# Packed queries times w_in in plain float32: eight side-by-side 64x32 tiles in place of three split products

## The chip, the cores and the metric

The kernel runs on one core of a Trainium2 chip (trn2). The metric is the device time of one launch in microseconds (us), taken as a median of several runs. The engines are named as in the profile: PE (TensorE matmuls), PEld (its weight loads), DVE (VectorE), ACT (ScalarE), POOL (GpSimd) and SP (SyncE, which issues all DMAs here).

## What is computed

```python
batch, n_heads, seq, head_dim, n_pack = 8, 8, 576, 64, 32          # d_model 512, d_ff 2048
def sm_attn(qq, kk, vv):
    s = scale * np.matmul(qq, kk.transpose(0, 1, 3, 2))
    a = np.exp(s - np.max(s, axis=-1, keepdims=True))
    a = a / (np.sum(a, axis=-1, keepdims=True) + 1e-09)
    return np.matmul(a, vv)
p_packed = sm_attn(p, k, v)                  # 32 packed queries per head
x = sm_attn(q, p_packed, p_packed)           # back to 576 rows per head
x = x.transpose(0, 2, 1, 3).reshape(4608, 512)
h = x @ w_in                                 # 512 x 2048
out = (0.5 * h * (1 + erf(h / sqrt(2)))) @ w_out
```

The weights arrive as 64-bit floating point numbers, so each 512-wide block of them is loaded as pairs of 32-bit words and put together on the chip ("decoded").

## The kernel before

Work goes by units. A unit u is one pair of batches (four pairs) and one 512-wide block of d_ff (four blocks), 16 units in all; u // 4 is the pair and u % 4 the block. The second attention's last product and w_in are joined the other way round: instead of (weights2 x p_packed) x w_in, the kernel first computes wp = p_packed x w_in, which has one row for each of 8 heads x 32 packed queries, and then h = wp-transposed-by-weights2 over those 256 rows. `hidden_steps` issues h in eight steps a unit (batch j = 0 or 1 of the pair, four 128-wide columns c), `gelu` evicts each and splits it, and `output_steps` multiplies it with w_out.

Most products run in TensorE's reduced float32 (F32R). So that no accuracy is lost, each operand is split into a high part (rounded to F32R) and a low part (the rest), and a product is made as three: high x high, high x low, low x high. `h` and `o` are of this kind. The attention scores (`products`, L483) are plain float32 in eight tiles of 64 rows by 32 columns of the array; unit 0's `wps` and `h` are plain float32 too.

For wp (`packed_w_in`), the packed queries of a head pair are laid out by `diagonals` in a 128x128 block-diagonal matrix `ph`, split by POOL (`packed_split`). Each unit has two groups (hh = 0, 1); a group makes, for two 128-row tiles of w_in, the three products of 512 columns, serves both batches of the pair at once, and lands in a two-bank PSUM tile of the ring `wide`. That ring holds two tiles, which `wps`, `h`, the scores and `o_edge` share. The result is evicted in four pieces of 64 rows by 512 columns: ACT casts a high part (L986), DVE subtracts it to get the low part (L990).

w_in is decoded in units 0 to 3, kept as a split tile `w` [128, 2, 512] (cast L935 on ACT, low part L884 on POOL), stored in DRAM (`ws`), and loaded again in units 4 to 15.

The order of all work is not the program's own: every operation is a generator step with a priority number and a cost, and `Order` runs a small model of the engines while the program is recorded, always issuing the ready operation with the lowest number. The tables FIRST (the first pair's attention and unit 0), LATER (the other three pairs) and LEAD hold these numbers. Before the first output product, the model fills PE's waits with dummy products (`keep_warm`, tile `idle<-still`), so that its clock stays up.

Of the kernel before, what the change touches and what calls it, by code (L numbers as in the profile page):

```python
# [10 lines left out]
F32 = mybir.dt.float32  # L11
F32R = mybir.dt.float32r
# [40 lines left out]
    "p": (-29.7, 4.9),  # L53
    "k": (11.1, 2.3, 11.3, 24.1),
    "v": (38.0, 41.0, 54.2, 58.2),
    "q": (26.8, 33.3, 45.5, 49.5),
    "scores1": (15.9, 4.7),
    "softmax1": (1.1, 16.6, -2.5, 19.8),
    "packed": (-28.0, 0.3, 2.2, 10.0),
    "scores2": (0.4, -12.1),  # L60
    "softmax2": (36.1, 29.5, 32.6, 41.4),
    "weights2": (25.3, 28.0, 35.5, 45.7),
# [4 lines left out]
LEAD = {"load": 4.4, "decode": -3.6, "packed_w_in": 4}  # L67

FIRST = {
    "p": (-200.0, -193.0),  # L70
    "k": (-186.0, -199.0, -185.0, -182.0),
    "v": (-195.0, -197.0, -181.0, -179.0),
    "q": (-183.0, -191.0, -178.0, -177.0),
    "w": (-187.0, -198.0, -194.0, -188.0, -192.0, -184.0, -190.0, -196.0, -189.0, -180.0, -176.0, -175.0),
    "scores1": (-29.0, -55.27, -22.89, -50.0),
    "softmax1": (-53.13, -50.0, -30.0, -29.0),
    "packed": (-48.76, -31.48, -27.58, -51.55),
    "scores2": (-51.65, -51.18, -34.07, -27.2),
    "softmax2": (-49.06, -48.66, -3.32, 1.29),
    "weights2": (-4.59, -15.04, -24.74, -16.37),  # L80
    "decode": (-45.0, -37.0, -20.64, -35.16, -36.53, -35.0, -50.97, -46.0, 1.0, 8.37, -33.0, 2.0),
    "packed_w_in": (-7.62, -48.76, -38.15, -25.99),
    "packed_split": (8.53, 1.15, 2.3, -11.78),
    "weights_split": (7.2, 1.11, -2.81, -0.07),
    "w_in_split": (-17.7, 3.0, 5.95, 3.0),
# [3 lines left out]
    "copy": ("DVE", "ACT", "DVE", "ACT", "ACT", "ACT", "DVE", "DVE"),  # L89
    "low": (0, 3, 4, 5),  # L90
    "banks": (False, False, False, False),
    "turn": {"k": ("ACT", "DVE", "ACT", "ACT"), "q": ("DVE", "DVE", "ACT", "ACT")},
# [42 lines left out]
class Op:  # L135
# [3 lines left out]
    def __init__(self, engine, cost, step, fn, takes=(), table=None, busy=True):  # L139
        self.engine, self.cost, self.step, self.fn = engine, cost, step, fn  # L140
        self.takes, self.table, self.busy = takes, table, busy


class Order:
# [4 lines left out]
    def __init__(self):  # L149
        self.now, self.serial, self.open = 0.0, 0, 0  # L150
        self.later, self.ready = [], {e: [] for e in (PE, ACT, DVE, POOL, DMA)}
        self.free = dict.fromkeys(self.ready, 0.0)
        self.table, self.link, self.under_way = None, DMA_FIRST, [0.0] * DMA_DEPTH
        self.warm, self.window, self.busy, self.idle = False, PE_WINDOW, 0.0, None
        self.free[PE] = PE_START
# [60 lines left out]
    def issue(self, engine):  # L216
# [23 lines left out]
        else:  # L240
            if op.table and op.table != self.table:
                self.table, begin = op.table, max(begin, self.free[engine] + TABLE_SWITCH)
            end = begin + op.cost
            if engine == PE:
                end = begin + self.clock(begin, op.cost, op.busy)
# [21 lines left out]
def packed_attention_gelu_ffn(ctx: ExitStack, tc: tile.TileContext, q, k, v, p, w_in, w_out, out):  # L267
# [40 lines left out]
    sms = ring("sm", 4, [P, S])  # L308
# [10 lines left out]
    wis = ring("wi", 4, [P, 2, FB], F32R)  # L319
    wos = ring("wo", 6, [P, 2, DM], F32R)  # L320
    wps = [ring("wp0", 1, [P, 2, 2, FB], F32R), ring("wp1", 2, [P, 2, 2, FB], F32R)]
# [6 lines left out]
    wos.names = [f"w_{u}_{i}" for u in range(NU) for i in range(4, 8)]  # L328
    gts.names = [f"g_{n}" for n in range(NU * 8)]
# [21 lines left out]
    ph = [const.tile([P, 2, 4 * P], F32R, name=f"ph{i}") for i in range(2)]  # L351
    for t in ph:
        nc.gpsimd.memset(t.bitcast(F32), 0.0)

    plain_ph = accs.take("ph")
    nc.gpsimd.memset(plain_ph, 0.0)


    pp_ready = {(b, hh): Event() for b in range(B) for hh in range(2)}
    plain_ready = {(b, hh): Event() for b in range(2) for hh in range(2)}  # L360
# [5 lines left out]
    a2T, plain_a2 = {}, {}  # L366
# [110 lines left out]
    def products(ts, lhs, rhs, swap=0):  # L477

        for n in range(2):
            rows = slice(64 * n, 64 * n + 64)  # L480
            for g in range(4):
                r0 = 32 * (g ^ 2 * swap)
                nc.tensor.matmul(  # L483
                    ts[n][r0:r0 + 32, :HALF], lhsT=lhs[n][rows, 32 * g:32 * g + 32], rhs=rhs(g)[rows],
                    start=True, stop=True)

    def scores_of_batch(bt, name, which, lhs, evacuate, engine, cost, step):
        xTs = [bt.xT[name, c].rearrange("p (g x) -> p g x", g=2) for c in range(2)]

        def part(half):  # L490
# [4 lines left out]
                    (t[:, 0], t[:, 1]), lhs, lambda g: xTs[g // 2][:, g % 2, cols], which == 2 and bt.j),  # L495
# [82 lines left out]
    def packed(s, step):  # L578
# [61 lines left out]
        s.ppT = yield Op(ACT, 0.16, step + 2, lambda t: nc.scalar.copy(t, bank(m)[:, :P]), [(ppts, f"ppT_{s.n}")])  # L640
        ring_.give(m)
        s.split = Event()
        if s.b < 2:
            yield Op(
                DVE, 0.2, step + 2,
                lambda: [nc.vector.tensor_copy(to[0], x) for to, x in diagonals(s, plain_ph.unsqueeze(1))])
            fire(plain_ready[s.b, s.hh])
            step = FIRST["packed_split"][s.i]
        start(packed_split(s, step + 2))

    def diagonals(s, base):

        j = s.bt.j
        for sel in range(2):
            rows = slice(64 * sel, 64 * sel + 64)
            yield [
                base[rows, part].rearrange("p (hh ea sel r) -> p hh ea sel r", hh=2, ea=4, sel=2)[
                    :, s.hh, j:4 - j:3 - 2 * j, sel] for part in range(base.shape[1])
            ], s.ppT[rows].rearrange("p (e sel r) -> p e sel r", e=2, sel=2)[:, :, sel]

    def packed_split(s, step):
        def fn():
            for (hi, lo), src in diagonals(s, ph[(s.b // 2) % 2]):
                nc.gpsimd.tensor_copy(hi, src)
                nc.gpsimd.tensor_tensor(lo, src, hi.bitcast(F32), ALU.subtract)

        yield Op(POOL, 1.4, step, fn)
        fire(s.split)
        fire(pp_ready[s.b, s.hh])

    def scores2_of_chunk(s, step):
# [4 lines left out]
            PE, 0.68, step, lambda *ts: products(banks(*ts), [s.ppT] * 2, lambda g: xT[:, g], s.bt.j), takes, busy=False)  # L676
        ts = ts if len(takes) > 1 else [ts]
        xts.give(s.bt.xT["q", s.hh])
        start(free_ppT(s))
# [9 lines left out]
    def scores2_of_batch(bt, step):  # L689
        for s in bt.chunks:  # L690
            s.e2 = yield Op(DVE, 0, step + 1, lambda t: None, [(sms, f"e2_{s.n}")])
        yield from scores_of_batch(
            bt, "q", 2, [s.ppT for s in bt.chunks],
            lambda s, cols, x: nc.vector.transpose(s.e2[:, cols], x), DVE, 0.74, step + 1)
        for s in bt.chunks:
            start(free_ppT(s))

    def free_ppT(s):
        yield s.split
        ppts.give(s.ppT)  # L700
# [19 lines left out]
    def softmax2(ss, step):  # L720
        n, m = len(ss), ss[0].mx2

        def centre(s):
# [3 lines left out]
                lambda: on(engine).tensor_tensor(u, u, per_block(m[:, 0, s.i]), ALU.subtract))  # L727
# [9 lines left out]
    def weights2(s, step):  # L737
# [8 lines left out]
        yield Op(engine, cost, step, lambda: on(engine).tensor_tensor(u, u, per_block(r), ALU.mult))  # L746
# [8 lines left out]
        else:  # L755
# [4 lines left out]
            engine, cost, step, lambda: on(engine).tensor_tensor(t[:, 1], raw, t[:, 0].bitcast(F32), ALU.subtract))  # L760
# [20 lines left out]

# [54 lines left out]
    def plain(u, i=0):  # L836

        return u == 0 and i < 4

    def parts_of(u, i=0):  # L840

        return 2 if plain(u, i) else 1

    w_ready = {(u, i, part): Event() for u in range(NU) for i in range(8) for part in range(parts_of(u, i))}
    wi_used = {(u, i): Event(0 if plain(u) else 1) for u in range(NU) for i in range(4)}
    plain_w, plain_used, plain_ph_used = {}, [Event(4) for _ in range(4)], Event(8)
    plain_ph_used.waiting.append(lambda: accs.give(plain_ph))
    stored = {(f, i): Event() for f in range(NF) for i in range(8)}
    wp_ready = {(u, j, part): Event(2) for u in range(NU) for j in range(2) for part in range(parts_of(u))}

    def weight_rows(f, i):

        if i < 4:
            return w_in[i * P:(i + 1) * P, f * FB:(f + 1) * FB]
        r0 = f * FB + (i - 4) * P
        return w_out[r0:r0 + P]

    def weight(u, i, load_steps, steps):
# [12 lines left out]
        t = home.get((u, i % 4))  # L871
        if plain(u, i):
            step, full = FIRST["w_in_split"][i], plain_w[i]
            t = home[u, i] = yield Op(ACT, 0.52, step, lambda d: nc.scalar.copy(d[:, 0], full), [(ring_, f"w_{n}")])
            yield from low_part(u, i, t, full, step)
            yield plain_used[i]
            accs.give(full)
        d = scratch[f, i] = dram.tile([P, 2, FB], F32, name=f"ws_{f}_{i}")
        start(keep(f, i, d, t, steps[-1] + 4))

    def low_part(u, i, d, full, step):
        engine, cost = (DVE, 0.6) if u == 0 and i in FIRST["low"] else (POOL, 1.23)
        yield Op(
            engine, cost, step, lambda: on(engine).tensor_tensor(d[:, 1], full, d[:, 0].bitcast(F32), ALU.subtract))  # L884

    def decode(u, i, part, load_step, step):
# [4 lines left out]
        raws = a2ts if plain(u, i) else wraws  # L891

        def words(t):
            if plain(u, i):
# [343 lines left out]
```

## Time and profile before

| | |
|---|---|
| median of 3 runs | 769.9 us (767.25 to 769.99) |
| the profiled execution: its time | 768.53 us |
| its span, first to last instruction | 766.7 us |
| mean granted PE clock | 0.996 |
| instructions in the profile | 12964 |
| bytes moved by DMA | 123.53 MB |

The span is cut by the views below into stretches in us from its start. "Busy" of PE counts each matmul from its start to a modelled end, and matmuls overlap: a PE that is 100% busy may still wait a little, and the spacing of starts says more than the length of one. A row of a timeline gives start, length, engine, line, operation, the tiles out<-in, their shapes and a count; a bracket gives the idle time before it and what ended that.

### The profile page before, as it was taken

The numbers are of one execution on the slowest core, as the hardware profiler recorded it, in microseconds if no ns is written. First come the engines' busy times: TensorE is split into PE (matmuls) and PEld (weight loads), VectorE is DVE, ScalarE is ACT, GpSimd is POOL, SyncE is SP. The second block draws the span as 40 slices with busy tenths as digits, with TensorE's granted clock in tenths as the row PEclk, the third lists the DMA queues.
The fourth block names the chain that finished last, engine by engine and source line by source line (L and its number), as shares of the span: only waits on it lengthen the run. The fifth ranks groups of instructions, "written<-read, shape, count | busy, mean of one in ns | idle before, by whom it ended". The sixth has DMA issues, their size and how long they took to land.

```text
span 766.7 us, 12964 instructions
## 1 busy us (share of the span) xinstructions
PE 743.2 (97%) x4948; PEld 621.5 (81%) x4948; DVE 458.5 (60%) x733; ACT 413.7 (54%) x714; POOL 204.7 (27%) x401
## 2 busy tenths in 40 slices
PE   9889998898999999999999999999999999999998
PEld 7667776676778888888778888888878888888886
DVE  5999767988787543446478643356479522352522
ACT  4888866859667254437447345336546354333421
POOL 3568535764541111111122111111122111111110
PEclk9999999999999999999999999999999999999999
DMA  9859995656744899334443799324542523222021
GB/s 301 301 205 208 219 275 187 232 183 172 273 142 164 206 160 223 127 125 100 144 142 141 183 193 214 148 103 94 170 144 110 190 98 116 103 97 72 6 105 69
DMA packets 159293, 123.53 MB, mean 161 GB/s; under 512 B 124416, under 2 KB 132608, under 8 KB 159232
## 3 DMA queue, kind: packets, MB, share of 16 engines
q1 hardware_dynamic: 159232, 122.71, 56.7%
q8 instruction: 39, 0.64, 0.4%
q14 instruction: 22, 0.18, 0.1%
HBM read 96.47 MB, written 26.21 MB: 160 GB/s over the span
## 4 chain that ended last, share of the span: by engine, by line
PE 77%; DVE 7%; DMA 6%; ACT 5%; SPq 2%; issue 1%; POOL 1%; ACTq 0%; POOLq 0%; DVEq 0%
PE h L1050 22%; PE o L1104 14%; PE o L1106 13%; PE o L1105 13%; DMA wraw<-in_moe_w_in_dram 2%; DMA wraw<-in_moe_w_out_dram 2%; DMA v<-in_v_dram 2%; PE o_edge L1104 2%; PE o_edge L1106 2%; PE o_edge L1105 2%; PE s L483 2%; PE wps L968 2%; PE wps L969 2%; PE wps L970 2%; ACT graw L1077 1%
## 5 line engine op out<-in xcount | busy, mean ns | idle before, releaser
L1077 ACT ACTIVATE graw<-h 128x576 f32<-128x576 f32 x128 | 102.4, 802 | 227.9 <-PE h L1050 173.4
L1050 PEld LDWEIGHTS h<-a2T,wp 128*128 128x128 f32 x1440 | 203.0, 189 | 15.1 <-DVE wp L990 2.6
L1050 PE MATMUL h<-a2T,wp 128*128 128x288 f32 x1440 | 211.6, 296 | 3.3 <-DVE wp L990 2.0
L1104 PE MATMUL o<-w,g 128*128 128x512 f32 x508 | 203.8, 401 | 0.9 <-ACT g L1083 0.9
L1106 PE MATMUL o<-w,g 128*128 128x512 f32 x508 | 199.8, 393 | 2.8 <-DVE g L1084 2.7
L1105 PE MATMUL o<-w,g 128*128 128x512 f32 x508 | 199.0, 392 | 0.0
L1084 DVE TENSOR_TENSOR g<-graw,g 128x512 fp32r<-128x512 f32 x128 | 96.5, 754 | 159.6 <-ACT g L1083 154.9
L1094 POOL CAST t<-graw 128x64 fp32r<-128x64 f32 x128 | 42.0, 328 | 434.9 <-ACT graw L1077 429.4
L1106 PEld LDWEIGHTS o<-w,g 128*128 128x128 f32 x508 | 95.9, 189 | 26.0 <-DVE g L1084 4.9
L1104 PEld LDWEIGHTS o<-w,g 128*128 128x128 f32 x508 | 96.1, 189 | 24.7 <-issue 6.0
L990 DVE TENSOR_TENSOR wp<-wps,wp 64x512 fp32r<-64x512 f32 x120 | 79.9, 687 | 50.1 <-ACT wp L986 48.7
L1105 PEld LDWEIGHTS o<-w,g 128*128 128x128 f32 x508 | 96.1, 189 | 16.5
L1165 DVE TENSOR_TENSOR acc<-o,acc 128x512 f32<-128x512 f32 x96 | 63.9, 685 | 35.8 <-PE o L1106 35.8
L1083 ACT CAST g<-graw 128x512 fp32r<-128x512 f32 x128 | 79.6, 623 | 2.6
L986 ACT CAST wp<-wps 64x512 fp32r<-64x512 f32 x120 | 66.7, 581 | 17.5 <-PE wps L970 16.4
L938 POOL TENSOR_TENSOR wt<-wt 128x512 int32<-128x512 int32 x28 | 38.0, 1359 | 39.9 <-DVE wt L922 39.9
L1095 POOL TENSOR_TENSOR t<-graw,t 128x64 fp32r<-128x64 f32 x128 | 45.8, 358 | 10.2
L906 ACT ACTIVATE wt<-wraw 128x512 f32<-128x512 f32 (+1 forms) x36 | 22.5, 626 | 28.5 <-DMA wraw<-in_moe_w_in_dram 15.7
L884 POOL TENSOR_TENSOR w<-wt,w 128x512 fp32r<-128x512 f32 x26 | 36.4, 1398 | 1.9 <-POOL wt L938 0.5
L412 DVE STREAM_TRANSPOSE kT<-k 128x1152 f32<-128x1152 f32 x12 | 16.5, 1376 | 21.5 <-DMA k<-in_k_dram 21.4
L922 DVE SCALAR_TENSOR_TENSOR wt<-wraw,wt 128x512 int32<-128x512 int32 (+1 forms) x36 | 26.6, 740 | 0.8
L1023 PE MATMUL idle<-still 128*128 128x256 bf16 x168 | 25.4, 294 | 1.5 <-DVE still L347 1.1
(139 smaller groups left out, 808.3 us busy)
## 6 DMA issues: line engine op xcount, KB each, us to landing
w<-ws SPq DMA_DIRECT2D x96, 512.0 KB, 5.0
ws<-w SPq DMA_DIRECT2D x32, 512.0 KB, 4.4
out_dram<-acc SPq DMA_DIRECT2D x36, 256.0 KB, 2.1
v<-in_v_dram SPq DMA_DIRECT2D x16, 512.0 KB, 5.2
wraw<-in_moe_w_out_dram SPq DMA_DIRECT2D x16, 512.0 KB, 5.0
k<-in_k_dram SPq DMA_DIRECT2D x48, 144.0 KB, 4.6
q<-in_q_dram SPq DMA_DIRECT2D x48, 144.0 KB, 5.1
wraw<-in_moe_w_in_dram SPq DMA_DIRECT2D x12, 512.0 KB, 4.3
```

Of the source, the lines that this page charges most:

```text
L986: (nc.vector.tensor_copy if engine == DVE else nc.scalar.copy)(hi.bitcast(F32) if plain(u) else hi, x)
L990: nc.vector.tensor_tensor(lo, x, hi.bitcast(F32), ALU.subtract)
L1050: nc.tensor.matmul(t[:, half, :HALF], lhsT=w[:, wpart, ch, fc], rhs=a2T[b, ch][:, apart, half * HALF:(half + 1) * HALF], start=ch == 0 and ...
L1077: lambda raw: nc.scalar.activation(*dst_src(raw), AF.Gelu), [(graws, f"graw_{n}")], table="gelu")
L1083: g = yield Op(ACT, 0.52, lead, lambda g: nc.scalar.copy(g[:, 0], main), [(gts, f"g_{n}")])
L1084: yield Op(DVE, 0.6, lead, lambda: nc.vector.tensor_tensor(g[:, 1], main, g[:, 0].bitcast(F32), ALU.subtract))
L1094: nc.gpsimd.tensor_copy(dst[:, 0], side)
L1095: nc.gpsimd.tensor_tensor(dst[:, 1], side, dst[:, 0].bitcast(F32), ALU.subtract)
L1104: nc.tensor.matmul(t, lhsT=g[0], rhs=w[:, 0], start=first, stop=False)
L1105: nc.tensor.matmul(t, lhsT=g[0], rhs=w[:, 1], start=False, stop=False)
L1106: nc.tensor.matmul(t, lhsT=g[1], rhs=w[:, 0], start=False, stop=last)
L1165: yield Op(DVE, 0.6, n, lambda: nc.vector.tensor_tensor(a, x, a, ALU.add))
```

## The change

w_in's product with the packed queries is made in plain float32 by the same `products` that makes the scores, now over 512 columns: eight matmuls of a 64x32 tile each, four heads of each half side by side. One group serves one batch j, so there are still two groups a unit, at different places in the order. With it:

- w_in is kept whole ([128, 512], no split), its rows are loaded in another order (`weight_rows`), and stores and reloads of it are half as large. Unit 0 no longer needs its extra float32 copy and the later split.
- The block-diagonal `ph`, its clearing, `diagonals` and `packed_split` go; ACT copies half a tile per chunk into `pp`. In the first pair DVE makes a second copy, `ppT`, for the second scores.
- The result is evicted in one piece of 128 rows by 1024 columns (one ACT cast, one DVE subtract).
- `wp1` has one buffer in place of two, `wi` six smaller ones, `sm` six in place of four.
- The planner gets a rule that POOL operations and some DVE operations exclude each other (`port`), and all three tables of numbers are new: every engine's order is remade. The second scores of the first pair now land in two one-bank tiles (`banks`).

```diff
-LEAD = {"load": 4.4, "decode": -3.6, "packed_w_in": 4}
+LEAD = {"load": 4.2, "decode": 1.5, "packed_w_in": 4.2}
...
-    "packed": (-48.76, -31.48, -27.58, -51.55),
+    "packed": (-17.05, -43.32, -29.01, -3.6),
...
+            if op.port:
+                begin = max(begin, self.port)
...
-    def products(ts, lhs, rhs, swap=0):
+    def products(ts, lhs, rhs, size=HALF):
         for n in range(2):
             rows = slice(64 * n, 64 * n + 64)
             for g in range(4):
-                r0 = 32 * (g ^ 2 * swap)
+                cols = slice(32 * g, 32 * g + 32)
                 nc.tensor.matmul(
-                    ts[n][r0:r0 + 32, :HALF], lhsT=lhs[n][rows, 32 * g:32 * g + 32], rhs=rhs(g)[rows],
-                    start=True, stop=True)
+                    ts[n][cols, :size], lhsT=lhs[n][rows, cols], rhs=rhs(g)[rows], start=True, stop=True)
...
-                base, w = ph[pr % 2][:, :, cut], wi[u, 2 * hh + e][:, :, cols]
-                nc.tensor.matmul(t[:, e, :m], lhsT=base[:, 0], rhs=w[:, 0], start=True, stop=False)
-                nc.tensor.matmul(t[:, e, :m], lhsT=base[:, 0], rhs=w[:, 1], start=False, stop=False)
-                nc.tensor.matmul(t[:, e, :m], lhsT=base[:, 1], rhs=w[:, 0], start=False, stop=True)
+            products((t[:, 0], t[:, 1]), [pp[b]] * 2, lambda g: wi[u, g][:, cols], m)
...
-        yield Op(engine, (0.32 + 0.75 * m / FB) * n, step, high)
-        for e in range(0 if plain(u) else 2):
-            yield Op(DVE, (0.07 + 0.58 * m / FB) * n, step, lambda: low(halves[n * e:n * e + n]))
+        yield Op(engine, 0.12 + 0.87 * m / FB, step, high)
+        if not plain(u):
+            yield Op(DVE, 0.1 + 1.1 * m / FB, step, lambda: nc.vector.tensor_tensor(lo, x, hi.bitcast(F32), ALU.subtract))
...
-            start(all_packed_w_in(u, (0, 1), [8 * u - LEAD["packed_w_in"]]))
+            for j in range(2):
+                start(packed_w_in(u, j, 0, 8 * u + 4 * j - LEAD["packed_w_in"]))
```

Three places of the order follow, as the recorded programs have it.

PE, unit 1's first group of wp, between output products of unit 0 (`o_4_..`). Before (the group's second half, with the next rows behind it):

```order
L968 MATMUL wps_1_1_0_0_1268<-w_1_2_1137,ph0_78 128x512
L969 MATMUL wps_1_1_0_0_1268<-w_1_2_1137,ph0_78 128x512
L970 MATMUL wps_1_1_0_0_1268<-w_1_2_1137,ph0_78 128x512
L968 MATMUL wps_1_1_0_0_1268<-w_1_3_1212,ph0_78 128x512
L969 MATMUL wps_1_1_0_0_1268<-w_1_3_1212,ph0_78 128x512
L970 MATMUL wps_1_1_0_0_1268<-w_1_3_1212,ph0_78 128x512
L1104 MATMUL o_4_2_1188<-w_0_5_644,g_5_1158 128x512
```

Now the whole group for batch 0 stands between two output products:

```order
L1050 MATMUL o_4_0_1200<-w_0_5_603,g_5_1117 128x512
L481 MATMUL wps_1_0_0_1242<-w_1_0_956,pp_0_399 32x512
L481 MATMUL wps_1_0_0_1242<-w_1_1_1079,pp_0_399 32x512
L481 MATMUL wps_1_0_0_1242<-w_1_2_1139,pp_0_399 32x512
L481 MATMUL wps_1_0_0_1242<-w_1_3_1216,pp_0_399 32x512
L1048 MATMUL o_4_1_1201<-w_0_5_603,g_5_1117 128x512
```

The four rows of the group stand there twice, once for each half of the array's rows; six matmuls on the whole array for each half of the heads have become eight on eighths of it, and batch 1's group follows later instead of being served at once.

DVE, the same unit's evictions. Before (`wp_1_0` and `wp_1_1` are the two batches' results; the four rows shown belong to the group's second half and stand behind four like them):

```order
L1084 TENSOR_TENSOR g_7_1266<-graw_7_1250,g_7_1266 128x512
L990 TENSOR_TENSOR wp_1_0_1071<-wps_1_0_0_0_1252,wp_1_0_1071 64x512
L990 TENSOR_TENSOR wp_1_1_1244<-wps_1_0_0_0_1252,wp_1_1_1244 64x512
L990 TENSOR_TENSOR wp_1_0_1071<-wps_1_1_0_0_1268,wp_1_0_1071 64x512
L990 TENSOR_TENSOR wp_1_1_1244<-wps_1_1_0_0_1268,wp_1_1_1244 64x512
L916 TENSOR_SCALAR wt_1_5_0_1347<-wt_1_5_0_1347 128x512
```

Now:

```order
L1027 TENSOR_TENSOR g_7_1232<-graw_7_1223,g_7_1232 128x512
L938 TENSOR_TENSOR wp_1_0_1144<-wps_1_0_0_1242,wp_1_0_1144 128x1024
L874 TENSOR_SCALAR wt_1_4_0_1251<-wt_1_4_0_1251 128x512
L875 TENSOR_SCALAR wt_1_4_0_1251<-wt_1_4_0_1251 128x512
L880 SCALAR_TENSOR_TENSOR wt_1_4_0_1251<-wraw_1_4_0_1156,wt_1_4_0_1251 128x512
```

A run of eight subtracts (each row above stands there twice) is now one, and decoding of the next weights (`wt_..`) follows it at once.

DVE ahead of the first h (`a2` is the transposed weights2 that the first h reads, `ph` the block-diagonal tile, `wp_0_0` unit 0's result for batch 0). Before:

```order
L646 COPY ph_82<-ppT_0_0_616 64x2x32 x2
L573 TENSOR_SCALAR st_1_0_513<-st_1_0_513 128x1
L574 RECIPROCAL st_1_0_513<-st_1_0_513 128x1
L557 TENSOR_SCALAR mx_0_85<-mx_0_85 128x1
L750 STREAM_TRANSPOSE a2_0_642<-e2_0_1_400 128x576
L986 COPY wp_0_0_92<-idle_621 64x256 x2
L573 TENSOR_SCALAR st_1_1_595<-st_1_1_595 128x1
L574 RECIPROCAL st_1_1_595<-st_1_1_595 128x1
L884 TENSOR_TENSOR w_0_5_644<-wt_0_5_0_432,w_0_5_644 128x512
L986 COPY wp_0_0_92<-wps_0_0_0_0_666 64x256 x2
```

Now:

```order
L570 TENSOR_SCALAR st_1_1_536<-st_1_1_536 128x1
L571 RECIPROCAL st_1_1_536<-st_1_1_536 128x1
L933 COPY wp_0_0_86<-idle_564 128x2x256
L719 STREAM_TRANSPOSE a2_0_742<-e2_0_0_503 128x576
L933 COPY wp_0_0_86<-wps_0_0_1_729 128x2x256
L643 COPY ppT_1_0_776<-ppTm_1_0_726 128x128
L874 TENSOR_SCALAR wt_0_7_0_750<-wt_0_7_0_750 128x512
```

The copies into `ph` and the low part of w_out (L884) have left DVE there, the half-height evictions are full ones, and a small copy of the packed queries (`ppT`) has come.

More of the change, by code (lines that the diff above doesn't have):

```diff
@@ L88 @@
     "gpsimd": (0, 1, 2, 3),
[L89 to L92, printed above, removed]
+    "copy": ("DVE", "DVE", "ACT", "DVE"),
+    "banks": (True, True, True, True),
+    "turn": {"k": ("DVE", "ACT", "ACT", "ACT"), "q": ("DVE", "ACT", "ACT", "ACT")},
 }
@@ L135, with __init__ @@
 class Op:
-    def __init__(self, engine, cost, step, fn, takes=(), table=None, busy=True):
+    def __init__(self, engine, cost, step, fn, takes=(), table=None, busy=True, port=False):
         self.engine, self.cost, self.step, self.fn = engine, cost, step, fn
         self.takes, self.table, self.busy = takes, table, busy
+        self.port = (engine == POOL and cost > 0) or port
 class Order:
@@ L318, in packed_attention_gelu_ffn @@
     wts = ring("wt", 2, [P, 2, FB], I32)
-    wis = ring("wi", 4, [P, 2, FB], F32R)
+    wis = ring("wi", 6, [P, FB])
     wos = ring("wo", 6, [P, 2, DM], F32R)
-    wps = [ring("wp0", 1, [P, 2, 2, FB], F32R), ring("wp1", 2, [P, 2, 2, FB], F32R)]
+    wps = [ring(f"wp{j}", 1, [P, 2, 2, FB], F32R) for j in range(2)]
+    pps = ring("pp", 4, [P, P])
     graws = ring("graw", 2, [P, S])
@@ L348, in packed_attention_gelu_ffn @@
     make_identity(nc, ident)
[L351 to L360, printed above, removed]
+    pp_ready = [Event(2) for _ in range(B)]
     a2_ready = [Event(2) for _ in range(B)]
@@ L639, in packed @@
         pns.give(pn)
-        s.ppT = yield Op(ACT, 0.16, step + 2, lambda t: nc.scalar.copy(t, bank(m)[:, :P]), [(ppts, f"ppT_{s.n}")])
-        ring_.give(m)
[L642 to L669, printed above, removed]
+        both = pp[s.b] = yield from one(pps, f"pp_{s.b}", ACT, step + 2)
+        rows = slice(64 * s.hh, 64 * s.hh + 64)
+        yield Op(ACT, 0.16, step + 2, lambda: nc.scalar.copy(both[rows], bank(m)[rows, :P]))
+        fire(pp_ready[s.b])
+        if s.b < 2:
+            s.ppT = yield Op(
+                DVE, 0.19, step + 2, lambda t: nc.vector.tensor_copy(t, bank(m)[:, :P]), [(ppts, f"ppT_{s.n}")])
+        ring_.give(m)
     def scores2_of_chunk(s, step):
@@ L870, in weight @@
         yield [decode(u, i, part, *at) for part, at in enumerate(zip(load_steps, steps))]
[L871 to L884, printed above, removed]
+        d = scratch[f, i] = dram.tile([P, FB] if i < 4 else [P, 2, FB], F32, name=f"ws_{f}_{i}")
+        start(keep(f, i, d, home[u, i % 4], steps[-1] + 4))
     def decode(u, i, part, load_step, step):
@@ L997, in packed_w_in @@
[L997 to L1004 removed]
+            products((t[:, 0], t[:, 1]), [pp[b]] * 2, lambda g: wi[u, g][:, cols], m)
+        t = yield Op(PE, 0.15 + 0.87 * m / FB, step, product, [(wide, f"wps_{u}_{j}_{part}")], busy=False)
@@ L1006, in free_wi, with all_packed_w_in @@
+        fire(wp_ready[u, j, part])
+        wide.give(t)
+        if u % NF == NF - 1:
+            pps.give(pp[b])
+    def all_packed_w_in(u, j, steps):
+        for part, step in enumerate(steps):
+            start(packed_w_in(u, j, part, step))
     def free_wi(u, i):
```

180 lines of the change are left out of this document (82 added, 98 removed).

## The prediction

> **What bounds the kernel now.** I read the page's busy lines first, then the stretches, the waits of PE, and last the timeline where a group of wp and a group of scores stand among other matmuls.
>
> ```profile
> PE 743.2 (97%) x4948; PEld 621.5 (81%) x4948; DVE 458.5 (60%) x733; ACT 413.7 (54%) x714; POOL 204.7 (27%) x401
> 20.00:40.00 20.00, 17.70 (x216) 13.39 (x215) 18.81 (x42) 16.70 (x39) 11.38 (x16) 1.00 0.75 271
> 40.00:57.00 17.00, 14.99 (x200) 10.29 (x199) 16.44 (x33) 13.85 (x32) 11.06 (x15) 1.00 0.61 218
> 57.00:240.00 183.00, 169.85 (x1080) 136.20 (x1080) 151.97 (x222) 138.42 (x219) 101.16 (x130) 0.98 0.75 210
> 400.00:500.00 100.00, 99.95 (x567) 86.62 (x566) 54.16 (x83) 48.17 (x81) 13.97 (x42) 1.00 0.74 169
> ```
>
> The columns of a stretch are its length, then busy us of PE, PEld, DVE, ACT and POOL (with instruction counts), the granted clock, the DMA share and GB/s. There are three regimes. Up to 57 us (the first h) DVE is the fullest engine, 35.25 of 37 us from 20 on; ACT has 30.55. From 57 to 240, while w_in and w_out are decoded, PE leads but is idle for 13.15 us, with DVE at 83% and ACT at 76%, and the clock is 0.98. Afterwards PE has no gap, and only PE work counts. What PE waits for after 60 us:
>
> ```profile
> PE e1Tm L585 <- ACT graw L1077: 3.6, 2, 2.3
> PE o L1106 <- DVE g L1084: 2.7, 3, 1.1
> PE h L1050 <- DVE wp L990: 2.0, 1, 2.0
> PE h L1050 <- ACT graw L1077: 1.0, 1, 1.0
> PE wps L968 <- ACT graw L1077: 0.9, 1, 0.9
> PE o L1104 <- ACT g L1083: 0.9, 1, 0.9
> PE idle L1106 <- DVE g L1084: 0.9, 1, 0.9
> ```
>
> These are 12.0 us in all (total, times, longest): a late gelu or its split, or a late wp. A wait on `graw` is one for a tile of the ring `wide`, which the gelu frees.
>
> **PE's part of the change.** Now six matmuls of a group's half cost this, shown by their starts:
>
> ```profile
> 458.84 0.39 PE L969 MATMUL wps<-w,ph 128*128 128x512 f32 x1
> 459.07 0.39 PE L970 MATMUL wps<-w,ph 128*128 128x512 f32 x1
> 459.30 0.40 PE L968 MATMUL wps<-w,ph 128*128 128x512 f32 x1
> 459.53 0.39 PE L969 MATMUL wps<-w,ph 128*128 128x512 f32 x1
> 459.76 0.40 PE L970 MATMUL wps<-w,ph 128*128 128x512 f32 x1
> 460.00 0.40 PE L1104 MATMUL o<-w,g 128*128 128x512 f32 x1
> ```
>
> Five starts in 1.16 us are 0.232 each; twelve a unit are 2.78, and 15 units 41.8 us. What takes their place has no row of its own, but the scores are the same eight tiles over 288 columns:
>
> ```profile
> 290.80 0.39 PE L1105 MATMUL o<-w,g 128*128 128x512 f32 x1
> 291.03 0.39 PE L1106 MATMUL o<-w,g 128*128 128x512 f32 x1
> 291.35 1.20 PE L483 MATMUL s<-kT,pT 64*32 64x288 f32 x32
> 292.48 0.50 PE L1104 MATMUL o<-w,g 128*128 128x512 f32 x1
> 292.82 0.40 PE L1105 MATMUL o<-w,g 128*128 128x512 f32 x1
> ...
> 381.60 0.27 PE L588 MATMUL e1Tm<-ident,e 128*64 128x128 f32 x1
> 381.80 0.72 PE L483 MATMUL s<-qT,ppT 64*32 64x288 f32 x16
> 382.45 0.50 PE L1104 MATMUL o<-w,g 128*128 128x512 f32 x1
> 382.78 0.39 PE L1105 MATMUL o<-w,g 128*128 128x512 f32 x1
> ```
>
> At 291 two groups (32 records; a float32 matmul leaves two) stand among output matmuls that start 0.23 apart. From the o at 291.03 to that at 292.82 are 1.79 us; without two o's (0.46) 1.33 remain. At 381 one group takes 382.78 - 381.60 = 1.18, less one o (0.23) and one small transpose (0.11): 0.84. So a second group adds 0.49, and going into and out of the tiles costs 0.35. The core grows with the columns: 0.49 x 512/288 = 0.87. A lone group of wp then takes 0.87 + 0.35 = 1.22, and 30 of them, which the new order puts at 30 separate places, 36.6 us. **The term is 36.6 - 41.8 = -5.2 us.** Its ends: -15.7 if the way in and out cost nothing (30 x 0.87), and +20.9 by the rival on halves below. I take the middle value since the row nearest in kind gives it.
>
> The Trainium skill, TensorEngine Tiling (Array Packing), section Tiling Modes, says that changing the tiling mode drains TensorE. That speaks against this change, which goes through a change of mode 60 times more; by the rule the term is -5.2, without it -15.7, and the 0.35 us of the rows above agree with it.
>
> Unit 0's four groups of 256 columns replace 16 matmuls, but ahead of the first h PE is filled with dummies, so I count nothing; if PE became the limit there, they would still be shorter.
>
> **The evictions, decoding and the rest.** These are the groups (busy us and mean ns of one):
>
> ```profile
> L990 DVE TENSOR_TENSOR wp<-wps,wp 64x512 fp32r<-64x512 f32 x120 | 79.9, 687 | 50.1 <-ACT wp L986 48.7
> L986 ACT CAST wp<-wps 64x512 fp32r<-64x512 f32 x120 | 66.7, 581 | 17.5 <-PE wps L970 16.4
> L986 DVE COPY wp<-wps 64x256 f32<-64x256 f32 x6 | 2.5, 422 | 0.1
> L986 ACT COPY wp<-wps 64x256 f32<-64x256 f32 x6 | 2.2, 366 | 1.3 <-PE wps L964 1.2
> L884 POOL TENSOR_TENSOR w<-wt,w 128x512 fp32r<-128x512 f32 x26 | 36.4, 1398 | 1.9 <-POOL wt L938 0.5 <-ACT w L935 0.4
> L935 ACT CAST w<-wt 128x512 fp32r<-128x512 f32 x28 | 17.6, 630 | 5.6 <-DVE wt L922 4.9 <-PE o_edge L1106 0.5
> L665 POOL TENSOR_TENSOR ph<-ppT,ph 64x64 fp32r<-64x64 f32 x32 | 11.7, 366 | 2.6
> L646 DVE COPY ph<-ppT 64x64 f32<-64x64 f32 x8 | 4.5, 569 | 0.1
> L427 DVE COPY qT<-qm 128x384 f32<-128x384 f32 x4 | 2.0, 545 | 0.0
> ```
>
> A piece of 1024 columns, by the slope from 256 to 512: ACT 581 + 2 x (581 - 366) = 1.01 us, DVE 687 + 2 x (687 - 422) = 1.22. Per unit ACT falls from 8 x 0.581 to 2 x 1.01 (-2.6), DVE from 8 x 0.687 to 2 x 1.22 (-3.1). From unit 4 on this is worth nothing: both engines are about half busy and PE does not wait.
>
> From 57 to 240, units 1 to 3 save 9.2 us of DVE and 7.9 of ACT; twelve casts of w_in (0.63) take 7.6 more off ACT, and twelve low parts (1.40) 16.8 off POOL, with 8 x 0.366 = 2.9 for the subtracts of one pair's `ph` and its casts besides. DVE would be at 78%, ACT at 67%. The wp that PE waited 2.0 us for would be evicted in 2.2 us instead of 4 x 0.581 + 4 x 0.687 = 5.1, and the tile of `wide` comes back sooner, which is what the waits on `graw` want. The waits are 12.0 us, and 0.02 x 183 = 3.7 of clock were lost. Ends: -15.7 if all go, +6 if the new order brings three more of the longest kind (2.0). I take half, **-8 us**, since 4.5 us of them are waits on g, whose cause, decoding ahead of it in the same queues, the change thins and does not remove.
>
> `wp1` with one buffer adds a wait: batch 1's group cannot be written before the previous unit's last h of batch 1. In the new order, the first h of batch 1 stands over 10 us of PE work behind its group in every unit, so the wait is covered. The tightest place is batch 0 of units 1 to 3: in unit 1, 24 output matmuls (24 x 0.23 = 5.5 us) for an eviction of 2.2; without that cover about 2 us each would be lost, in the +6 above.
>
> Up to 57 us, DVE loses `ph` (4.5), three low parts of about 0.7 ahead of the first h (2.2), six half-height copies (2.5) and three copies of qT that ACT gets (1.6). It gains at most three wp copies of 0.422 + 0.265 = 0.69 (2.1) and four copies `ppT` of 0.29 (by the same slope, 1.2). That is -7.5 net. ACT is late next: it loses six wp copies (2.2) and four casts of w_in (2.5), gains three copies of qT and one of wp (2.2), and an earlier decode of unit 1's w_in (two activations, 1.3), so stays near 29.4 of the 37 us. DVE at 27.8 and ACT at 29.4 wait for one another more. **I take -4 us**, about half of the relief; ends -7.5 and +5, the landing time of a late load:
>
> ```profile
> v<-in_v_dram SPq DMA_DIRECT2D x16, 512.0 KB, 5.2
> w<-ws SPq DMA_DIRECT2D x96, 512.0 KB, 5.0
> ws<-w SPq DMA_DIRECT2D x32, 512.0 KB, 4.4
> ```
>
> for the new order puts four half-size stores of w_in between the first pair's loads in SP's queue, each of which waits for decoding. Later, 48 reloads and 16 stores of half the size take 64 x 0.26 = 17 MB off; no row of PE's waits above is a DMA, so they count nothing.
>
> **The sum.** 768.5 (the profiled execution: span 766.7 and 1.8 around it) - 5.2 - 8 - 4 = 751.3. The median shown is 1.4 us higher, so I say 752.
>
> **Rivals.**
> 1. *Only PE's term comes.* The remade order ends up with as much waiting as the old: 768.5 - 5.2 = 763. For it: the waits hang on gelu, g and decoding, which stay. Against: every engine but PE has less to do there.
> 2. *No net gain.* The first h is 5 us later (a load behind a store), which eats PE's term: 768. For it: the loads of the first pair stand in another order, and SP's queue is strict. Against: DVE, not DMA, is full there.
> 3. *The tiles do not all run side by side at 512 columns* (slower): if the array's two row halves went one after the other, a group takes 2 x 0.87 + 0.35 = 2.09, PE's term is 62.7 - 41.8 = +20.9, and the time is 777. It decides from 1.9 us a group on. Against: at 381 sixteen records begin within 0.65 us. For: no row has eight tiles with 512 columns. The Trainium skill, FP8 and Floating Point Precision, section TensorE Precision Notes, says that true FP32 makes four passes through the array; that agrees with 0.49 us for 288 columns, and is why this rival is dear.
> 4. *All of the relief arrives*: waits gone and DVE's 7.5 us: 768.5 - 5.2 - 15.7 - 7.5 = 740.
>
> **Chances.** The sum 0.60 (own range 745 to 760); rival 1 0.20, most of it faster; rival 2 0.07; rival 3 and other new waits 0.06; rival 4 0.07. No change means within 0.5% (766 to 774), about what a measurement here can tell. Faster: 0.60 + 0.17 + 0.07 = 0.84; same: 0.03 + 0.07 = 0.10; slower 0.06. A range from 743 to 768 leaves out rival 3 and most of rival 4, some 0.13.
>
> **What would show it.** Right: 16 records of wp in about 1.0 us with the next o some 0.1 late; ACT and DVE pieces of 1024 columns near 1.0 and 1.2; first h between 50 and 55 us; waits of PE after 60 us near 6 us, clock 1.00. Wrong: records of a group beginning in two clumps 0.9 apart; a first h after 57; new waits of PE on wp or on POOL's `w`, or further clock dips between 60 and 240 us.

## The result, and the profile after

The changed kernel takes 881.9 us (median of 4 runs, 879.6 to 883.8), the kernel before 769.6 us beside it (767.3 to 770.0). The ratio is 1.147, with a 95% interval of 1.143 to 1.151: 112 us slower, where I had forecast 17 us faster. The profiled execution has a span of 877.8 us.

The page of the changed kernel, busy times and four of the rows in 40 slices (a slice is 22 us):

```profile
PE 765.8 (87%) x5288; PEld 606.3 (69%) x5288; DVE 398.6 (45%) x627; ACT 370.2 (42%) x604; POOL 161.4 (18%) x322
PE   5547686964796699999999999989999999999998
DVE  1336463732473578534456345344654442133333
PEclk7768788986897699999999999999999999999999
DMA  3574366952431254599513135997040432403012
```

Everything that was to get lighter did: DVE went from 458.5 to 398.6 us of work, ACT from 413.7 to 370.2, POOL from 204.7 to 161.4. And yet in the first fourteen slices, some 310 us, PE has gaps, its clock is down, and no other engine is full. The right half of the page looks like the kernel before. An unfilled PE with unfilled helpers means that they wait for one another or for something outside, so the waits come next: the largest of PE, then the one of ACT on the loads of w_in.

```profile
PE idle L421 <- DMA k<-in_k_dram: 16.5, 3, 9.1
PE ppTm L634 <- ACT pn L627: 10.8, 2, 7.4
PE idle L620 <- DMA v<-in_v_dram: 8.5, 1, 8.5
PE idle L458 <- DMA p<-in_p_dram: 8.3, 1, 8.3
PE o L1048 <- ACT acc L1105: 8.1, 1, 8.1
```

```profile
ACT wt L864 <- DMA wraw<-in_moe_w_in_dram: 123.4, 19, 10.7
```

Three of PE's are DMAs now: k, v and p, which the change does not touch (in the kernel before, PE's waits on them are 0.6 us for p and 0.2 for v). Behind ACT's row stands the larger thing. ACT's first decoding steps wait 123.4 us for w_in in 19 pieces; in the kernel before the same wait was 15.7 us in 9:

```profile
ACT wt L906 <- DMA wraw<-in_moe_w_in_dram: 15.7, 9, 4.6
```

ACT's start in the changed kernel, four decoding steps of unit 0's w_in (256 columns each; the bracket is the idle time before it):

```profile
9.09 0.43 ACT L864 ACTIVATE wt<-wraw 128x256 f32<-128x256 f32 x1 [6.86 <-DMA wraw<-in_moe_w_in_dram]
15.54 0.43 ACT L864 ACTIVATE wt<-wraw 128x256 f32<-128x256 f32 x1 [5.70 <-DMA wraw<-in_moe_w_in_dram]
22.38 0.43 ACT L864 ACTIVATE wt<-wraw 128x256 f32<-128x256 f32 x1 [4.96 <-DMA wraw<-in_moe_w_in_dram]
28.30 0.43 ACT L864 ACTIVATE wt<-wraw 128x256 f32<-128x256 f32 x1 [5.17 <-DMA wraw<-in_moe_w_in_dram]
```

A load of 256 KB becomes ready every 6.4 us ((28.30 - 9.09) / 3), which is about 41 GB/s. What the DMA engines do meanwhile is seen in a stretch of 3 us, first of the changed kernel, then of the kernel before (columns as in the prediction; the last three are the clock, the DMA share and GB/s):

```profile
10.00:13.00 3.00, 2.57 (x12) 2.37 (x13) 0.59 (x2) 0.00 (x0) 0.72 (x1) 0.50 0.14 52
```

```profile
10.00:13.00 3.00, 3.00 (x39) 2.11 (x37) 2.10 (x6) 0.93 (x4) 0.81 (x2) 1.00 1.13 314
```

0.14 of 16 engines is 2.2 engines. In the kernel before all sixteen count as busy there, and they move six times as much. The code that sets this is `weight_rows`, of which I had said only that it loads "in another order":

```diff
-    def weight_rows(f, i):
+    def weight_rows(f, i, cols):
         if i < 4:
-            return w_in[i * P:(i + 1) * P, f * FB:(f + 1) * FB]
+            rows = w_in.rearrange("(hh g d) n -> g hh d n", hh=2, g=4)
+            return rows[i, :, :, f * FB + cols.start:f * FB + cols.stop]
```

Each load of w_in was one DMA over 128 rows; it is one DMA over 2 blocks of 64 rows, and its outermost dimension is 2. The Trainium skill, DMA: Bandwidth & Descriptors, section Rules for kernel authors, says that a DMA whose outermost dimension has c < 16 entries is confined to at most c engines. The trace agrees: its 2.2 counts all transfers of the stretch, not those of w_in alone.

A slow load is not alone in the queue. SP's issues of the changed kernel (start, length of the issuing instructions, x2 where two stand together):

```profile
2.55 4.15 SPq L384 DMA_DIRECT2D k<-in_k_dram  x1
6.74 6.27 SPq L858 DMA_DIRECT2D wraw<-in_moe_w_in_dram  x2
13.05 6.63 SPq L452 DMA_DIRECT2D p<-in_p_dram  x2
```

The changed kernel's first three issues, ahead of these, take 0.42 to 0.69 us, and the kernel before issues such a k in 0.46. The same issue of k takes 0.58 us in the first experiment below, which has the same order and another form of the loads. Here the issues shown take 3.1 to 4.2 us each on average, and SP issues in a fixed order, so k, p and v are late, and what reads them.

Where the 122 us between the profiled changed kernel and the same kernel with this one thing mended (the first experiment, span 755.7) went can be added up. The first h begins at 97.6 us in place of 53.1: 44.5 us. From the first h on:

```profile
97.60:400.00 302.40, 239.78 (x1481) 184.77 (x1475) 155.42 (x230) 147.18 (x219) 83.68 (x119) 0.88 0.55 135
400.00:877.80 477.80, 469.10 (x3198) 381.91 (x3196) 205.30 (x311) 188.77 (x308) 55.11 (x176) 1.00 0.40 105
```

```profile
53.10:755.70 702.60, 686.70 (x4669) 553.09 (x4669) 364.15 (x542) 336.41 (x527) 139.05 (x296) 0.99 0.53 130
```

PE is idle for 62.6 + 8.7 = 71.3 us against 15.9, which is 55.4 more. Its busy time is 708.9 against 686.7 for the same work, 22.2 more. That is what the clock accounts for, by an estimate: 0.12 of the 240 us in the first stretch are 29, less 7 for 0.01 of the 687 of the mended kernel. 44.5 + 55.4 + 22.2 = 122.1. How much of it comes from w_in itself being late, and how much from the loads held up behind it, was not separated.

### The profile page after: what moved, and what is told of

Read it like the earlier page. It is cut to its first block, busy times and chain, and to the rows that moved or that the text cites. A ratio compares the mean times of both kernels' runs of the same rounds, so it can differ in the third digit from the quotient of the medians.

```text
span 877.8 us, 13293 instructions
## 1 busy us (share of the span) xinstructions
PE 765.8 (87%) x5288; PEld 606.3 (69%) x5288; DVE 398.6 (45%) x627; ACT 370.2 (42%) x604; POOL 161.4 (18%) x322
## 4 chain that ended last, share of the span: by engine, by line
PE 59%; DMA 10%; DVE 4%; ACT 2%; SPq 1%; issue 1%; DVEq 0%; ACTq 0%
PE h L992 17%; PE o L1048 11%; PE o L1050 10%; PE o L1049 10%; DMA wraw<-in_moe_w_in_dram 7%; PE wps L481 3%; DMA k<-in_k_dram 2%; SPq L394 1%; PE o_edge L1048 1%; PE o_edge L1050 1%; PE o_edge L1049 1%; PE s L481 1%; DVE g L1027 1%; PE pp L620 1%; DMA wraw<-in_moe_w_out_dram 1%
## 5 line engine op out<-in xcount | busy, mean ns | idle before, releaser
L992 PE MATMUL h<-a2T,wp 128*128 128x288 f32 x1440 | 215.6, 300 | 15.2 <-ACT graw L1019 7.2
L992 PEld LDWEIGHTS h<-a2T,wp 128*128 128x128 f32 x1440 | 208.0, 193 | 26.4 <-ACT pp L639 7.7
L1048 PE MATMUL o<-w,g 128*128 128x512 f32 x508 | 212.6, 418 | 14.3 <-ACT acc L1105 8.1
L1050 PE MATMUL o<-w,g 128*128 128x512 f32 x508 | 203.8, 401 | 1.6 <-DVE g L1027 1.4
L1049 PE MATMUL o<-w,g 128*128 128x512 f32 x508 | 202.7, 399 | 0.0
L1048 PEld LDWEIGHTS o<-w,g 128*128 128x128 f32 x508 | 98.3, 194 | 64.9 <-issue 24.5
L1050 PEld LDWEIGHTS o<-w,g 128*128 128x128 f32 x508 | 97.9, 193 | 25.3 <-DVE g L1027 2.7
L1049 PEld LDWEIGHTS o<-w,g 128*128 128x128 f32 x508 | 98.4, 194 | 15.6
L1109 DVE TENSOR_TENSOR acc<-o,acc 128x512 f32<-128x512 f32 x96 | 62.6, 684 | 32.6 <-PE o L1050 32.5
L864 ACT ACTIVATE wt<-wraw 128x512 f32<-128x512 f32 (+1 forms) x36 | 22.3, 618 | 128.2 <-DMA wraw<-in_moe_w_in_dram 123.4
L874 DVE TENSOR_SCALAR wt<-wt 128x512 f32<-128x512 f32 (+1 forms) x36 | 17.7, 490 | 92.9 <-ACT wt L864 92.9
L938 DVE TENSOR_TENSOR wp<-wps,wp 128x1024 fp32r<-128x1024 f32 x30 | 36.5, 1218 | 22.8 <-ACT wp L933 22.8
L933 ACT CAST wp<-wps 128x1024 fp32r<-128x1024 f32 x30 | 30.3, 1011 | 31.6 <-PE wps L481 31.6
L889 POOL TENSOR_TENSOR w<-wt 128x512 int32<-128x512 int32 (+1 forms) x20 | 22.9, 1143 | 112.7 <-DVE wt L880 94.4
L481 PE MATMUL wps<-w,pp 64*32 64x512 f32 (+1 forms) x528 | 35.3, 595 | 0.1
L965 PE MATMUL idle<-still 128*128 128x256 bf16 x176 | 30.5, 333 | 1.1 <-DVE still L354 1.1
```

Of the source, the lines that this page charges most:

```text
L481: nc.tensor.matmul(ts[n][cols, :size], lhsT=lhs[n][rows, cols], rhs=rhs(g)[rows], start=True, stop=True)
L938: yield Op(DVE, 0.1 + 1.1 * m / FB, step, lambda: nc.vector.tensor_tensor(lo, x, hi.bitcast(F32), ALU.subtract))
L992: nc.tensor.matmul(t[:, half, :HALF], lhsT=w[:, wpart, ch, fc], rhs=a2T[b, ch][:, apart, half * HALF:(half + 1) * HALF], start=ch == 0 and ...
L1048: nc.tensor.matmul(t, lhsT=g[0], rhs=w[:, 0], start=first, stop=False)
L1049: nc.tensor.matmul(t, lhsT=g[0], rhs=w[:, 1], start=False, stop=False)
L1050: nc.tensor.matmul(t, lhsT=g[1], rhs=w[:, 0], start=False, stop=last)
```

## The experiments

**1. The changed kernel, with each load of w_in as two DMAs of 64 rows** (`two_dmas`). Nothing else in it differs: the planner, the order and the bytes are the same.

```diff
+        def fetch(dst, src):
+            if i < 4:
+                for hh in range(2):
+                    nc.sync.dma_start(dst[64 * hh:64 * hh + 64], src[hh])
+            else:
+                nc.sync.dma_start(dst, src)
...
-            lambda t: nc.sync.dma_start(
-                words(t).rearrange("p n t -> p (n t)"), weight_rows(f, i, cols).bitcast(I32)),
+            lambda t: fetch(words(t).rearrange("p n t -> p (n t)"), weight_rows(f, i, cols).bitcast(I32)),
```

> The changed kernel with each of its 20 loads of w_in issued as two DMAs of 64 rows each, nothing else changed (the planner's numbers and so every engine's order stay). Theory A: the single DMA, whose destination is written as two blocks of 64 rows, is moved by two of the 16 DMA engines only (about 24 packets of 2 KB start per us at 85 ns each while one is under way), so a 512 KB load takes 10 us instead of 4, delays everything queued behind it, and the rest of the change is as forecast: 740 to 765 us, first h before 60 us, PE clock 0.99 or more. Theory B: the remade order, not the form of the load, makes the waits (loads of k, p and v stand later in SP's queue): still over 850 us. Theory C, between: both; 780 to 850 us.

Measured: 761.6 us (757.4 to 763.8), ratio 0.989 to the kernel before (0.986 to 0.993). So 120 us of the changed kernel's time hang on the form of 20 DMAs (both versions read the same rows from the same places), and the rest of the change is a gain of 1.1%. This version beats both kernels. The same stretch, the landing time of its half loads (KB each, median us), and ACT's wait:

```profile
10.00:13.00 3.00, 3.00 (x27) 2.57 (x26) 1.83 (x5) 1.66 (x5) 0.66 (x1) 1.00 1.12 290
```

```profile
wraw<-in_moe_w_in_dram SPq DMA_DIRECT2D x24, 256.0 KB, 4.6
```

```profile
ACT wt L870 <- DMA wraw<-in_moe_w_in_dram: 10.6, 9, 2.8
```

**2. The kernel before, with only this form of load put in** (`before_2engines`). If the form is enough by itself, it must spoil a kernel that has nothing else of the change.

```diff
-            return w_in[i * P:(i + 1) * P, f * FB:(f + 1) * FB]
+            rows = w_in.rearrange("(hh g d) n -> g hh d n", hh=2, g=4)
+            return rows[i, :, :, f * FB:(f + 1) * FB]
...
```

> The kernel before, with only its 20 loads of w_in given the changed kernel's row order and form (one DMA of two blocks of 64 rows). It leaves out the right order of w_in's rows in the products, so its output is not the reference's; all instructions keep their shapes. Theory A: 8 loads of 128 x 2 KB and 12 of 128 x 4 KB on two engines, 8 x 5.4 + 12 x 10.2 = 166 us of them, mostly in the first 200 us: slower by 60 to 120 us, 830 to 890 us. Theory B: within 10 us of 769.

Measured: 888.8 us (887.4 to 889.7), ratio 1.155 (1.153 to 1.157). The form alone costs 120 us in either kernel, and is sufficient as well as necessary.

**3. Only unit 0's eight loads mended** (`two_dmas_unit0`): `if i < 4:` becomes `if i < 4 and u == 0:`.

> The changed kernel with two DMAs for each of unit 0's eight loads of w_in only; the twelve larger loads of units 1 to 3 stay single. Theory A: the first h comes before 60 us instead of at 97.6, the rest of the loss stays: 882 - 40 = about 840 us (820 to 855). Theory B: 870 us or more.

Measured: 848.3 us (847.9 to 849.1), ratio 1.103 (1.101 to 1.105). The first h comes at 62.0 us instead of 97.6, but the end only 34 us earlier. The three units after it, 12 loads of twice the size, carry the other 87 us of the 120; it is not a matter of the start alone.

**4 and 5. The kernel before, with the loads in 4 blocks of 32 rows and in 16 blocks of 8** (`hh=4` and `hh=16` in the edit of experiment 2). Two theories stood: that the count of outermost blocks sets how many engines work, or that the scattered rows themselves are slow.

> The kernel before with its 20 loads of w_in as one DMA of four blocks of 32 rows each (rows in another order, so its output is not the reference's). Theory A, an outermost dimension of n blocks is moved by n engines: four engines, a 512 KB load in some 5 to 6 us, half the serial time of the two-block form (83 us in place of 166, against a baseline that has about 40 of its own): 775 to 815 us. Theory B, what costs is that the rows of a load do not follow one another in DRAM: as the two-block form, 889 us or more.

> As before_4engines, with 16 blocks of 8 rows each (output not the reference's either). Theory A: all 16 engines, 769 us within 0.5%. Theory B: 889 us or more.

Measured: 817.9 us (ratio 1.063, 1.061 to 1.065) and 774.3 us (1.0056, 1.0038 to 1.0074). The first is 3 us above what I had given, the second 5 us above the kernel before. ACT's wait for w_in with 2, 4 and 16 blocks:

```profile
ACT wt L907 <- DMA wraw<-in_moe_w_in_dram: 129.1, 18, 11.6
```

```profile
ACT wt L907 <- DMA wraw<-in_moe_w_in_dram: 67.2, 15, 7.5
```

```profile
ACT wt L907 <- DMA wraw<-in_moe_w_in_dram: 16.0, 8, 5.3
```

Twice the blocks, half the wait; with sixteen it is that of the kernel before (15.7). The first h comes at 100.9, 78.3, 60.0 us (before: 57.0). With sixteen blocks the rows are scattered more than with two, so scatter can be charged with the last 5 us at most.

**6. The mended kernel, with both batches' groups of wp next to each other from unit 3 on** (`two_dmas_pairs`): 60 trips into and out of the tiles would become fewer, and `wp1` gets its second buffer back.

```diff
-                start(packed_w_in(u, j, 0, 8 * u + 4 * j - LEAD["packed_w_in"]))
+                start(packed_w_in(u, j, 0, 8 * u - LEAD["packed_w_in"]))
...
-    wps = [ring(f"wp{j}", 1, [P, 2, 2, FB], F32R) for j in range(2)]
+    wps = [ring(f"wp{j}", 1 + j, [P, 2, 2, FB], F32R) for j in range(2)]
```

> As two_dmas, with both batches' groups of wp at one place in the order from unit 3 on (13 units) and two buffers for wp1. If going into and out of the tiles costs 0.35 us, each adjoining pair saves it once: 13 x 0.35 = 4.6 us less than two_dmas, if the altered order brings no waits. If the way in and out costs nothing, no difference.

Measured: 766.2 us (764.3 to 769.2), ratio 0.997 (0.995 to 0.998), 4.6 us slower than experiment 1 where I expected 4.6 faster. The saving on PE is there at the places compared. A lone group in experiment 1, with an undisturbed piece behind it, and then a pair in this kernel:

```profile
652.48 1.75 PE L998 MATMUL h<-a2T,wp 128*128 128x288 f32 x12
654.15 1.09 PE L481 MATMUL wps<-w,pp 64*32 64x512 f32 x16
655.17 0.50 PE L1054 MATMUL o<-w,g 128*128 128x512 f32 x1
655.51 0.39 PE L1055 MATMUL o<-w,g 128*128 128x512 f32 x1
...
658.03 1.75 PE L998 MATMUL h<-a2T,wp 128*128 128x288 f32 x12
659.61 0.40 PE L1054 MATMUL o<-w,g 128*128 128x512 f32 x1
659.85 0.39 PE L1055 MATMUL o<-w,g 128*128 128x512 f32 x1
```

```profile
661.24 1.75 PE L998 MATMUL h<-a2T,wp 128*128 128x288 f32 x12
662.91 1.96 PE L481 MATMUL wps<-w,pp 64*32 64x512 f32 x32
664.80 0.50 PE L1054 MATMUL o<-w,g 128*128 128x512 f32 x1
665.13 0.39 PE L1055 MATMUL o<-w,g 128*128 128x512 f32 x1
```

From the start of the twelve h's to the second o: 3.03 us with one group, 1.82 with none, 3.89 with two. One costs 1.21, two 2.07. So the core of a group is 0.86 and the way in and out 0.35. But new waits paid more than that back:

```profile
PE h L998 <- ACT graw L1025: 5.9, 3, 2.9
PE s L481 <- DVE wp L944: 4.8, 2, 2.8
PE e1Tm L582 <- ACT graw L1025: 3.4, 1, 3.4
```

In experiment 1 the first two are not in the list and the third is 1.9. 12.2 us of new waits came (5.9 + 4.8 + 1.5), and 4.1 us on pT and kT went. That the planner moved other operations with the second batch's group is likely and was not followed further. The two profiles also differ by 2.9 us before the first h (56.0 us here, 53.1 in experiment 1), in an order that the edit leaves as it is.

**7. The mended kernel with less DVE work** (`two_dmas_light`). The prediction put PE's remaining waits down to decoding ahead of g. This one leaves out two of the DVE steps of decoding (the clamp and the shift) in units 1 to 3.

```diff
-            nc.vector.tensor_scalar(t.bitcast(F32), t.bitcast(F32), W_LEAST, W_MOST, ALU.max, ALU.min)
-            nc.vector.tensor_scalar(t, t, 3, 0x3FFFFFF8, ALU.logical_shift_left, ALU.bitwise_and)
+            if u == 0:
+                nc.vector.tensor_scalar(t.bitcast(F32), t.bitcast(F32), W_LEAST, W_MOST, ALU.max, ALU.min)
+                nc.vector.tensor_scalar(t, t, 3, 0x3FFFFFF8, ALU.logical_shift_left, ALU.bitwise_and)
```

> two_dmas without the two DVE instructions that clamp and shift each decoded tile in units 1 to 3 (28 tiles, 56 instructions, about 1.0 to 1.3 us a tile, some 30 us of DVE; weights of these units come out wrong). If the waits of PE that stayed in two_dmas between 57 and 240 us are due to DVE's decoding work, as the prediction assumed for half of them, they fall and the time goes down by 4 to 9 us against two_dmas, to 753 to 758. If they come from the order and from late inputs, within 2 us of two_dmas.

Measured: 760.6 us (759.3 to 762.2), ratio 0.988 (0.986 to 0.990): 1 us from experiment 1, within its spread. The stretch of decoding in experiment 1, and here:

```profile
57.00:240.00 183.00, 177.35 (x1220) 139.67 (x1219) 142.09 (x209) 129.95 (x192) 78.13 (x103) 0.98 0.74 178
```

```profile
57.00:240.00 183.00, 176.23 (x1219) 138.80 (x1218) 115.34 (x165) 130.01 (x192) 76.37 (x103) 0.99 0.73 178
```

DVE has 26.8 us less to do and PE gains nothing. My reason for the remaining waits falls. PE's waits on g, 4.5 us of those that the prediction listed, were down to 0.6 in experiment 1 already; the ones that stayed are others (experiment 8).

**8. The mended kernel with k loaded three steps earlier** (`two_dmas_k_early`). The waits that were left included scores on a late kT.

```diff
-    "k": (19.3, 8.3, 28.1, 6.4),
+    "k": (16.3, 5.3, 25.1, 3.4),
```

> two_dmas with the loads of k for the later pairs put three steps earlier in the planner's table (about 13 us). In two_dmas the scores of the later pairs wait for the transposed k (1.2 to 1.7 us each time beside the normal spacing, near 266, 278, 443 and 455 us). If late k is the cause, these waits go: 3 to 6 us less than two_dmas, so 756 to 759. If not, within 2 us of it.

Measured: 760.8 us (756.8 to 763.8), ratio 0.988 (0.983 to 0.992), the same as experiment 1. The waits that it was to take away, in experiment 1 and here:

```profile
PE s L481 <- DVE pT L464: 2.9, 2, 1.5
PE e1Tm L582 <- ACT graw L1025: 1.9, 1, 1.9
PE s L481 <- ACT graw L1025: 1.8, 2, 1.0
PE s L481 <- DVE kT L410: 1.2, 1, 1.2
```

```profile
PE s L481 <- DVE pT L464: 3.8, 2, 2.5
PE s L481 <- DVE kT L410: 1.3, 1, 1.3
```

They stand as they did. This does not clear the load of k, though, for the edit did not bring k in sooner where it matters. Here are the transposes of k on DVE ahead of the waits near 268 and 280 us, in experiment 1 and then here, with the copy of pT behind the second:

```profile
266.59 1.38 DVE L410 STREAM_TRANSPOSE kT<-k 128x1152 f32<-128x1152 f32 x1 [3.18 <-DMA k<-in_k_dram]
...
277.73 1.38 DVE L410 STREAM_TRANSPOSE kT<-k 128x1152 f32<-128x1152 f32 x1 [5.40 <-DMA k<-in_k_dram]
...
279.60 0.42 DVE L464 COPY pT<-pTm 128x256 f32<-128x256 f32 x1
```

```profile
267.13 1.38 DVE L410 STREAM_TRANSPOSE kT<-k 128x1152 f32<-128x1152 f32 x1 [3.19 <-DMA k<-in_k_dram]
...
279.40 1.38 DVE L410 STREAM_TRANSPOSE kT<-k 128x1152 f32<-128x1152 f32 x1 [6.54 <-DMA k<-in_k_dram]
```

In both, DVE sits idle until k lands, and the transposes begin no earlier. Even less the 2.5 us by which this execution is behind from its first h on (55.6 against 53.1), they are at most 2 us sooner, not 13. The scores wait for kT, or for pT, whose copy stands behind a transpose and a piece of g in DVE's order; the wait near 457 us has the same form, with DVE idle for 5.54 us until k lands. So late k does stand behind these 4.1 us (2.9 + 1.2) in experiment 1. Why its loads did not come sooner, and what the time would be if they did, is open.

## Why the prediction was wrong

**The step that failed is a term that the sum did not have.** It priced what the edits do to engines, and said of DMAs: "no row of PE's waits above is a DMA, so they count nothing". That sentence was about fewer bytes, where it may stand, and about a list that began at 60 us, while 8 of the 20 loads belong to unit 0. But the change also gave the 20 loads of w_in another form, and I had it in front of me as "its rows are loaded in another order" and never asked what a load of that form costs. It is worth +120 us (experiments 1 and 2), seven times the whole forecast. Two things hid it. A wait that is absent in the trace of before says that a transfer is in time as it is; it does not bound what the transfer costs once it is changed. And the row that did bear on it, ACT's wait of 15.7 us for w_in, did not enter it, since ACT was not the engine that bounds. None of the four rivals had the mechanism either; "a load behind a store" was priced at 5 us.

The other terms can be judged on experiment 1, which has them all. Its profiled execution takes 757.4 us, 11.1 below the 768.5 that the sum started from; its median is 7.2 below the median beside it.

- **PE's term: right.** Predicted 0.87 + 0.35 = 1.22 us for a lone group and -5.2 us; measured 0.86 + 0.35 = 1.21, which makes 30 x 1.21 - 41.8 = -5.5. Rival 3 falls: 16 records of wp take 1.09 us, so the eight tiles run side by side at 512 columns too.
- **Evictions: right.** Predicted 1.01 us on ACT and 1.22 on DVE for 1024 columns. The groups of the changed kernel:

```profile
L938 DVE TENSOR_TENSOR wp<-wps,wp 128x1024 fp32r<-128x1024 f32 x30 | 36.5, 1218 | 22.8 <-ACT wp L933 22.8
L933 ACT CAST wp<-wps 128x1024 fp32r<-128x1024 f32 x30 | 30.3, 1011 | 31.6 <-PE wps L481 31.6
```

- **The start: right in this execution.** Predicted -4 and a first h between 50 and 55 us; it begins at 53.1, against 57.0 before: -3.9. But the profiles of experiments 6, 7 and 8, with the same order up to there, have it at 56.0, 54.0 and 55.6. What the traces show is a gain of 1 to 4 us, and this profile has the best of it.
- **The waits: mis-sized.** Predicted -8. In the stretch from 57 to 240 PE's idle time fell from 13.15 to 5.65 us, which is -7.5. But it did not stay: after 240, where "PE does not wait" had been true of the old order, the new one has waits of scores for pT, kT and graw of 4.9 us, the drain at the end is 1.4 us longer, and the clock over 57 to 240 is 0.98 as before. What is left is 7.5 - 4.9 - 1.4, about -1, and -5.5 - 3.9 - 1 makes -10.4 of the 11.1. By the medians, 3 to 4 us less of the gain remains; the spread of the first h, up to 2.9 us, may be most of that. The reason that I gave, decoding ahead of g on DVE, is refuted by experiment 7; 4.1 of the 4.9 us are waits behind late loads of k (experiment 8).
- **`wp1` with one buffer: covered**, as predicted. PE's waits of experiment 1 after 57 us have none on wp.

With the loads mended, the likeliest sum (752) would have been 10 us too low at the median, and rival 1 ("only PE's term", 763) the nearest. Its ground, about as much waiting as before, is what the trace of experiment 1 shows; that its number fits so well is partly luck, since it leaves out the gain at the start.

## What to carry to other kernels

When a diff touches the access pattern of a DMA, price that DMA as a new operation, even if no engine waited for the old one: count the entries of its outermost dimension first, and if there are fewer than there are DMA engines, split it into several DMAs or order the pattern with the long dimension outside (the latter was not run here in the changed kernel). The sign of it is a profile in which all engines are half empty, with waits on loads that the change did not touch, and stretches in which the DMA share is near 2/16: here 0.14 from 10 to 13 us, while other transfers bring 17 of the first 20 slices of the page to 0.3 or more. And look at the engines that consume a load, not only at the one that bounds. ACT's 15.7 us of waiting on these loads in the kernel before, in 9 pieces, say that about half of the 20 had no slack there; with two blocks that wait grew to 129.1 us.

## What the hardware showed that I had not expected

- Loads of 2 x 64 rows came in at 256 KB every 6.4 us, with 0.14 of the DMA engines' time in use from 10 to 13 us, though four of them had been issued by 13 us and only one had come in: several such loads in flight did not spread over more engines. The same bytes as two DMAs land in 4.6 us (median of the 256 KB halves). In the kernel before, 2, 4 and 16 blocks give 889, 818 and 774 us, and one dimension of 128 rows 769.
- A load on few engines holds up the issuing engine also: with the same order of issues, the second load of k took 0.58 us to issue where w_in's loads are two DMAs each and 4.15 where they are one, and a load of p 3.3 us. So the loads of other tensors came late.
- PE's granted clock was low where PE had gaps, and full where it was busy: 0.88 over the stretch from 97.6 to 400 us, where PE was 79% busy, and 1.00 afterwards, where it was 98% busy. By the estimate above, that made the same matmuls some 22 us longer, a fifth of the loss, on top of the waits.
